# Gate and value products of a fused attention + SwiGLU kernel by Strassen's scheme

## The chip, the cores and the metric

The kernel runs on one core of a Trainium2 chip. The metric is the device time of one execution in microseconds. Engines are named as in the profile: PE (TensorE matmuls), PEld (its weight loads), DVE (VectorE), ACT (ScalarE), POOL (GpSimd), SP (SyncE, which here issues transfers).

## What is computed

Softmax attention over 8 batches of 12 heads, 448 tokens and 64 features a head, and behind it a SwiGLU block on all 3584 tokens:

```python
scores = q @ k.T / sqrt(64);  attn = softmax(scores) @ v       # per batch and head
x   = attn, heads side by side                                 # [3584, 768]
g   = x @ w_gate                                               # [768, 1536]
val = x @ w_val                                                # [768, 1536]
out = (g * sigmoid(g) * val) @ w_out                           # [1536, 768], f32 result
```

Inputs are f32; the matmuls work on f16 copies and accumulate in f32.

## The kernel before

**Attention.** Two heads make a pair; there are 48 pairs, six to a batch. The features of q and k lie on partitions (64 a head), so a score product uses half of the array's rows and the two heads of a pair sit on the two halves (tile shape 64x128 in the profile). One *unit* is one score tile of a pair for all 448 queries: two matmuls into a two-bank PSUM tile `s`, then one exp on ACT (L283), 128x896. From pair 12 on a pair has three units of 128 keys, and the 64 keys left over of two pairs share one unit (`RU`, L275, four 64x64 matmuls). The value product (`pv_mm`, L356) takes the exponentials as weights and V with a column of ones as moving operand, 65 columns; the left-over keys use 64 rows. DVE divides (L397, L398) into `xt`, and two DMA transposes on SP write the batch's columns of `X` (features on partitions, tokens along).

**SwiGLU.** For each of 12 feature tiles of 128 (`ffn1_steps`), six matmuls make the gate `gp` and six the value `vp` (L469), moving up to 512 tokens. ACT takes Tanh of half the gate (L492), DVE forms (tanh + 1) * gate (L499) and the gated product `hts` in f16 (L502). `ffn2_steps` multiplies chunks of 128 tokens by `w_out` in two halves of 384 columns, twelve matmuls each (L525); ACT evicts (L532) and SP stores. Token blocks are of 384 and 512 tokens by turns, so that all chunks are full: block 2k holds the first 384 tokens of two batches, block 2k+1 the other 512.

**PSUM.** `ps_s` has three two-bank tiles, shared by scores and gates; `ps_f` has two one-bank tiles, shared by values, value-product accumulators and output products.

**Order.** Everything is issued in one order written out by hand (`tc.manual_schedule`), and each engine works through its queue in that order. A loop over `plan` makes visits. A visit issues up to three score units in a row, then the left-over part of the value product of a pair whose units are done, for both heads, then the rest of it, and then the feature tiles and output steps due at that visit. Weights and q, k, v come through POOL's queue, cast to f16 on the way.

Of the kernel before, what the change touches and what calls it, by code (L numbers as in the profile page):

```python
# [17 lines left out]
NB = 2  # L18
# [3 lines left out]
RB = 5  # L22
# [11 lines left out]
LAST = 2  # L34
# [3 lines left out]
def kernel(  # L38
# [43 lines left out]
    raws = ctx.enter_context(tc.tile_pool(name="raws", bufs=2))  # L82
# [3 lines left out]
    fp = ctx.enter_context(tc.tile_pool(name="fp", bufs=3))  # L86
    ps_s = ctx.enter_context(tc.tile_pool(name="ps_s", bufs=3, space=PSUM))
    ps_f = ctx.enter_context(tc.tile_pool(name="ps_f", bufs=2, space=PSUM))

    Ebuf = [consts.tile([128, (NC * EB + 1) * D], FP16, name=f"E{i}") for i in range(NE)]  # L90
    Es = [e[0:P].rearrange("p (b x) -> p b x", x=D) for e in Ebuf]
    Eq = [e[:, 0 : NC * EC].rearrange("p (c x) -> p c x", c=NC) for e in Ebuf]
    Xts = [consts.tile([128, 8, D], FP16, name=f"xt{i}") for i in range(NX)]
    Vts = [consts.tile([128, 2, NC, D + 2], FP16, name=f"vo{i}") for i in range(NV)]
    vraw = consts.tile([128, VS, 2, NC, D], FP16, name="vraw")
    warm = consts.tile([128, 512], FP16, name="warm")
# [9 lines left out]

    wo = [consts.tile([128, NFB, OH], FP16, name=f"wo{i}") for i in range(2)]
# [5 lines left out]
    def dummy(n):  # L113
        wp = ps_f.tile([128, 512], FP32, tag="f", name="wp")
        for _ in range(n):
            nc.tensor.matmul(wp[:], lhsT=warm[:, 0:128], rhs=warm[:], start=True, stop=True)  # L116

    def load_qk32(pr):
        rq = raws.tile([P, 2, NC, D], FP32, tag="rq", bufs=RB)
        rk = raws.tile([P, 2, NC, D], FP32, tag="rk", bufs=RB)  # L120
        for dst, src in ((rq, q), (rk, k)):
            nc.sync.dma_start(dst[:], src[0, 2 * pr : 2 * pr + 2].rearrange("h (p c) d -> p h (c d)", c=NC))
        raw[pr] = (rq[:], rk[:])

    pairbuf = []
# [10 lines left out]


    def load_qk16(pr, n=2):
        h0 = 2 * (pr % 2) if pr >= 14 else 0
        if h0 == 0:  # L140
            q16 = raws.tile([128, 4, NC, D], FP16, tag="rq", bufs=RB, name="q16")
            k16 = raws.tile([128, 4, NC, D], FP16, tag="rk", bufs=RB, name="k16")
            pairbuf[:] = [q16, k16]
        q16, k16 = pairbuf
        for dst, src in ((q16, q), (k16, k)):
            if pr >= QUAD and dst is k16:
                kd = k16[:, ds(h0, 2 * n)].rearrange("p h c d -> p h (c d)")
                load_keys(nc.gpsimd, kd, k, 2 * pr, 2 * n)
                continue
            flat = src.rearrange("b h s d -> (b h) s d")[2 * pr : 2 * pr + 2 * n]  # L150
            nc.gpsimd.dma_start(dst[0:P, ds(h0, 2 * n)], flat.rearrange("h (p c) d -> p h (c d)", c=NC))  # L151
        for i in range(n):
            h = h0 + 2 * i
            raw[pr + i] = (q16[0:P, h : h + 2], k16[:, h : h + 2] if pr >= QUAD else k16[0:P, h : h + 2])
# [101 lines left out]

    def qk_quad(pr, c):
        s = ps_s.tile([128, 2, 512], FP32, tag="s")
        if c < KR:
# [9 lines left out]
            e = Eq[pr % NE][:, c]  # L269
        else:  # L270
# [11 lines left out]
            e = Eq[pr % NE][:, RU]  # L282
# [64 lines left out]
    def pv_mm(pr, hx, c, j):  # L347
        lo = low(pr, hx)
        first = not accs[pr][1][hx]
        accs[pr][1][hx] += 1  # L350
        if c < KR:
            rows, e, col = slice(0, 128), Eq[pr % NE][:, c], c + lo
        else:
            rows, col = (slice(0, 64), 0) if lo else (slice(64, 128), KR)
            e = Eq[(pr - pr % 2) % NE][:, RU]
        nc.tensor.matmul(  # L356
            accs[pr][0][hx][:, ts(j, D + 1)],
            lhsT=e[rows, ds(hx * S + j * 128, 128)],
            rhs=Vts[pr % NV][rows, hx, col, 0 : D + 1],
            start=first,  # L360
            stop=accs[pr][1][hx] == (KR + 1) ** 2,
        )

    def wide(pr):
        return pr >= NPAIR - LAST

    def pv_open(pr):
        if pr not in accs:
            if wide(pr):
                acc = ps_s.tile([128, 2, 512], FP32, tag="s", name="acc")  # L370
                accs[pr] = ([acc[:, 0], acc[:, 1]], [0, 0], acc)
            else:
                accs[pr] = ([ps_f.tile([128, 512], FP32, tag="f", name="acc"), ps_f.tile([128, 512], FP32, tag="f", name="acc")], [0, 0])

    def pv_piece(pr, c, heads=(0, 1)):
        pv_open(pr)
        for j in range(KR + 1):
            for hx in heads:
                pv_mm(pr, hx, c, j)

    def pv_close(pr):
        xt = Xts[pr % NX][:].rearrange("p (s h) d -> p s h d", h=2)
        if wide(pr):
            a4 = accs[pr][2][:, :, 0 : (KR + 1) * (D + 1)].rearrange("p h (s d) -> p h s d", s=KR + 1)
            r = attp.tile([128, 2, KR + 1], FP32, tag="R", bufs=4, name="R")
            nc.vector.reciprocal(r[:], a4[:, :, :, D])
            nc.vector.tensor_tensor(
                xt.rearrange("p s h d -> p h s d"),
                a4[:, :, :, 0:D],
                r[:].unsqueeze(3).to_broadcast([128, 2, KR + 1, D]),  # L390
                ALU.mult,
            )
            return
        for hx in range(2):
            a4 = accs[pr][0][hx][:, 0 : (KR + 1) * (D + 1)].rearrange("p (s d) -> p s d", s=KR + 1)
            r = attp.tile([128, KR + 1], FP32, tag="R", bufs=4, name="R")
            nc.vector.reciprocal(r[:], a4[:, :, D])  # L397
            nc.vector.tensor_tensor(  # L398
                xt[:, :, hx],
                a4[:, :, 0:D],  # L400
                r[:].unsqueeze(2).to_broadcast([128, KR + 1, D]),
                ALU.mult,
            )

    def pv_quad(pr):
        for hx in range(2):
            for c in range(KR):
                pv_piece(pr, c, (hx,))
        pv_close(pr)
# [53 lines left out]

    def ffn1_steps(kk, c0, n, hts, late=None):
        for fb in range(NFB):
# [25 lines left out]
            sg = fp.tile([128, 512], FP32, tag="sg")  # L491
# [6 lines left out]
            t1 = fp.tile([128, 512], FP32, tag="t1")  # L498
# [5 lines left out]
            )  # L504
            yield

    def ffn2_steps(kk, c0, n, hts, first, last_block):
# [6 lines left out]
        for ch, oh in steps:  # L514
# [7 lines left out]
            for m0, w in parts:  # L522
# [14 lines left out]
                l0 = c0 + ch * 128  # L537
                l = l0
                while l < l0 + 128:
                    b, j = divmod(l, S)  # L540
                    turned = D if b + NB * kk < QUAD // NHP else 0
                    c, p0 = divmod((j + turned) % S, P)
                    m = min(P - p0, l0 + 128 - l, (MQ if turned and j < MQ else S) - j)
                    eng = nc.scalar if last and m < 64 else nc.sync
                    eng.dma_start(
                        out[ts(NB * kk + b, S), :].rearrange("(p c) m -> c p m", c=NC)[
                            c, p0 : p0 + m, ds(m0, w)
                        ],
                        osb[l - l0 : l - l0 + m, ds(m0, w)],
                    )  # L550
                    l += m
            yield NFB * OH / 2400.0

    def block(i):
        kk, odd = divmod(i, 2)
        c0, n = (384, 512) if odd else (0, 384)
        hts = hp_.tile([128, NFB, 512], FP16, tag="h")
        late = (lambda: turn_x(FIRST - 1)) if i == 0 else None
        return ffn1_steps(kk, c0, n, hts, late), ffn2_steps(kk, c0, n, hts, i == 0, i == B - 1), n

    with tc.manual_schedule():
        load_qk32(0)
        nc.vector.memset(warm[:], 0.0)
        for e, eq in zip(Es, Eq):
            nc.vector.memset(eq[:, :, 2 * S :], 1.0)
            nc.vector.memset(e[:, 7::EB], 0.0)
        for vo in Vts:
# [159 lines left out]
        for x, (chunks, todo) in enumerate(plan):  # L727
# [3 lines left out]
            for _, p0 in todo:  # L731
                if p0 >= QUAD:
                    pv_piece(p0, RU)
# [37 lines left out]
            if adds[max(y for y in adds if y <= x)] < 2:  # L771
                if bare and oq and not fvq:
                    carry -= run_o()
                elif bare:
                    gate_small[0] = True
                carry = run_budget(left() / (end - x) + carry)
            else:
                nf, no = steps.pop(0) if steps else (0, 0)
                if bare and no:
                    run_o()  # L780
                    no -= 1
                elif bare:
                    gate_small[0] = True
                for y in range(nf):
                    if fvq:
                        run_fv()
                for _ in range(no):
                    run_o()
# [7 lines left out]
        oq.extend(ffn2_wait)  # L796
        ffn2_wait.clear()
        for _ in range(3):
            run_o()
        add_block(B - 1, 1)  # L800
        run_budget(1e9)
        oq.extend(ffn2_wait)
        run_budget(1e9)
# [30 lines left out]
```

## Time and profile before

| | |
|---|---|
| three timed runs | 451.52, 452.60, 452.68 us; median 452.6 |
| span of the profiled execution | 448.9 us, first to last instruction |
| between span and median | 3.7 us (launch and end; the profiled execution's own time is not listed apart) |
| PE busy | 438.8 us, 4024 matmuls |
| ACT, DVE, POOL busy | 224.9, 198.2, 180.3 us |
| gate and value matmuls (L469), output matmuls (L525) | 1152 and 684 |
| HBM read, written | 49.55 MB, 11.01 MB |

Rows of the page's groups read: line, engine, operation, output tile <- input tiles, for PE the array's tile shape (rows*columns), shape and type, count | busy us of the group, mean ns of one | idle time of the engine before them and what ended it. Matmuls are pipelined, so their mean durations overlap; what one costs in a dense stream is the distance from one start to the next. In the timeline a row is: start us, us from the first start to the last end, engine, line, operation, count.

### The profile page before, as it was taken

Reading aid. Unit: us, or ns where it says so; the run is one execution under the profiler, and the core shown is the slowest. Engines: PE = TensorE matmul, PEld = TensorE weight load, DVE = VectorE, ACT = ScalarE, POOL = GpSimd, SP = SyncE. Lnnn points to the kernel's source line nnn. Section 1 sums busy time; section 2 is a strip of 40 time slices with the busy share of each in tenths; the row PEclk is TensorE's granted clock in tenths of the full one; section 3 lists DMA queues with packets and bytes.
Section 4 is the critical chain, followed back from the end, with each engine's and each line's share of the span. In section 5 each row is a group of like instructions: output and inputs, shape, how many; then the busy total and the mean of one; then the engine's idle time right before and its main releaser. Section 6 shows DMA issues by size and latency. Waiting matters only on the chain.

```text
span 448.9 us, 9960 instructions
## 1 busy us (share of the span) xinstructions
PE 438.8 (98%) x4024; PEld 246.7 (55%) x4024; DVE 198.2 (44%) x447; ACT 224.9 (50%) x332; POOL 180.3 (40%) x299
## 2 busy tenths in 40 slices
PE   8999999899999999999999999999999999999996
PEld 3666565544455566554556556554455656644464
DVE  4666562364664354344445444343444434044400
ACT  6965666546554654455445465454454552222222
POOL 8755715997784483336444267423000000000000
PEclk9999999999999999999999999999999999999999
DMA  9999999999999799965899697955151211200033
GB/s 135 187 200 201 198 179 144 138 179 208 128 146 95 124 156 123 126 111 66 105 114 119 103 141 102 149 91 84 32 79 47 55 38 22 85 22 1 0 107 105
DMA packets 108494, 49.90 MB, mean 111 GB/s; under 512 B 60832, under 2 KB 104992, under 8 KB 108448
## 3 DMA queue, kind: packets, MB, share of 16 engines
q0 software_dynamic: 46832, 24.56, 47.6%
q1 hardware_dynamic: 61520, 24.66, 30.8%
q8 instruction: 31, 0.51, 0.5%
q14 instruction: 15, 0.12, 0.1%
q10 hardware_dynamic: 96, 0.05, 0.0%
HBM read 49.55 MB, written 11.01 MB: 135 GB/s over the span
## 4 chain that ended last, share of the span: by engine, by line
PE 76%; DMA 13%; DVE 3%; POOL 3%; ACT 2%; issue 1%; SPq 0%; DVEq 0%; POOLq 0%
PE op L525 22%; PE gp L469 22%; PE vp L469 19%; PE acc L356 8%; DMA k<-in_k_dram 5%; DMA wv<-in_moe_w_val_dram 4%; PE s L262 4%; DMA wg<-in_moe_w_gate_dram 2%; DMA qkT<-qk 2%; DVE t L499 1%; DVE hts L502 1%; ACT sg L492 1%; PE s L275 1%; ACT E L301 1%; PE wp L116 1%
## 5 line engine op out<-in xcount | busy, mean ns | idle before, releaser
L469 PE MATMUL gp<-X,wg 128*128 128x384 f16 (+1 forms) x576 | 124.8, 352 | 0.0
L469 PE MATMUL vp<-X,wv 128*128 128x384 f16 (+1 forms) x576 | 124.8, 352 | 0.0
L525 PE MATMUL op<-wo,hts 128*128 128x384 f16 (+1 forms) x684 | 115.5, 323 | 0.4 <-DVE xt L398 0.4
L283 ACT ACTIVATE E<-s 128x896 f16<-128x896 f32 x126 | 106.5, 922 | 14.9 <-PE s L262 8.7
L499 DVE SCALAR_TENSOR_TENSOR t<-sg,gp 128x384 f32<-128x384 f32 (+1 forms) x96 | 59.6, 621 | 111.7 <-ACT sg L492 111.7
L492 ACT ACTIVATE sg<-gp 128x384 f32<-128x384 f32 (+1 forms) x96 | 52.6, 548 | 92.1 <-PE gp L469 90.6
L525 PEld LDWEIGHTS <-hts 128*128 128x128 f16 x684 | 65.9, 98 | 45.6 <-issue 2.2
L469 PEld LDWEIGHTS <-wv 128*128 128x128 f16 x576 | 56.3, 98 | 52.5
L532 ACT ACTIVATE osb<-op 128x384 f32<-128x384 f32 (+1 forms) x57 | 27.6, 485 | 102.5 <-PE op L525 98.6
L469 PEld LDWEIGHTS <-wg 128*128 128x128 f16 x576 | 53.3, 98 | 45.5 <-issue 0.7
L502 DVE SCALAR_TENSOR_TENSOR hts<-t,vp 128x384 f16<-128x384 f32 (+1 forms) x96 | 59.6, 621 | 10.8 <-PE rtp L453 0.5
L188 POOL COPY qk<-k 128x512 f16<-128x512 f16 x36 | 22.9, 636 | 97.9 <-DMA qkT<-qk 95.7
L132 POOL DMA_DIRECT2D vraw<-in_v_dram x72 | 43.9, 634 | 15.2 <-DMA k<-in_k_dram 7.5
L397 DVE RECIPROCAL R<-acc 128x4 f32<-128x4 f32 x68 | 12.0, 177 | 73.9 <-PE acc L356 73.9
L356 PE MATMUL acc<-vo,E 128*128 128x65 f16 (+1 forms) x1152 | 43.0, 193 | 1.7 <-DVE hts L502 1.4
L301 ACT ACTIVATE E<-s 112x896 f16<-112x896 f32 x48 | 40.6, 916 | 7.9 <-PE s L293 7.8
L356 PEld LDWEIGHTS <-E 128*128 128x128 f16 (+1 forms) x1152 | 37.2, 96 | 12.8 <-issue 7.1
L132 POOL DMA_DIRECT2D k<-in_k_dram x70 | 42.5, 624 | 1.4 <-DMA wv<-in_moe_w_val_dram 0.8
L151 POOL DMA_DIRECT2D q<-in_q_dram x44 | 29.9, 680 | 4.7 <-PE s L293 1.5
L398 DVE TENSOR_TENSOR xt<-acc,R 128x256 f16<-128x256 f32 x68 | 28.9, 424 | 2.3
L262 PE MATMUL s<-qkT 64*128 64x448 f16 x216 | 28.1, 353 | 0.5 <-DMA qkT<-qk 0.5
L188 POOL COPY qk<-q 112x512 f16<-112x512 f16 x36 | 23.0, 639 | 0.0
(56 smaller groups left out, 184.4 us busy)
## 6 DMA issues: line engine op xcount, KB each, us to landing
vraw<-in_v_dram POOLq DMA_DIRECT2D x72, 64.0 KB, 4.7
q<-in_q_dram POOLq DMA_DIRECT2D x41, 112.0 KB, 4.0
k<-in_k_dram POOLq DMA_DIRECT2D x68, 64.0 KB, 4.7
wg<-in_moe_w_gate_dram POOLq DMA_DIRECT2D x8, 288.0 KB, 9.5
wv<-in_moe_w_val_dram POOLq DMA_DIRECT2D x8, 288.0 KB, 10.0
wo<-in_moe_w_out_dram POOLq DMA_DIRECT2D x2, 1152.0 KB, 19.8
out_dram<-osb SPq DMA_DIRECT2D x8, 288.0 KB, 3.5
out_dram<-osb SPq DMA_DIRECT2D x6, 336.0 KB, 2.9
```

The lines of the kernel that those rows point to most:

```text
L132: eng.dma_start(dst[ts(s, 64)], rows)
L151: nc.gpsimd.dma_start(dst[0:P, ds(h0, 2 * n)], flat.rearrange("h (p c) d -> p h (c d)", c=NC))
L188: nc.gpsimd.tensor_copy(dst.rearrange("p c h d -> p h c d"), src)
L262: nc.tensor.matmul(s[:, hx, 0:S], lhsT=t[ts(hx, 64), ts(c + low(pr, hx), 128)], rhs=t[ts(hx, 64), ds(NC * 128, S)], start=True, stop=True,)
L283: nc.scalar.activation(e[:, 0 : 2 * S].rearrange("p (h q) -> p h q", h=2), s[:, :, 0:S], AF.Exp, scale=sm_scale)
L301: nc.scalar.activation(e[:, :, 0:S], s[0:P, :, 0:S], AF.Exp, scale=sm_scale)
L356: nc.tensor.matmul(accs[pr][0][hx][:, ts(j, D + 1)], lhsT=e[rows, ds(hx * S + j * 128, 128)], rhs=Vts[pr % NV][rows, hx, col, 0 : D + 1], ...
L469: nc.tensor.matmul(dst[:, 0:n], lhsT=wslice(kind, fb, cb), rhs=X[kk][:, cb, ds(c0, n)], start=(cb == 0), stop=(cb == NCB - 1),)
L492: nc.scalar.activation(sg[:, 0:n], gp[:, 0:n], AF.Tanh, scale=0.5)
L499: nc.vector.scalar_tensor_tensor(t1[:, 0:n], sg[:, 0:n], 1.0, gp[:, 0:n], ALU.add, ALU.mult)
L502: nc.vector.scalar_tensor_tensor(hts[:, fb, 0:n], t1[:, 0:n], 0.5 * HS, vp[:, 0:n], ALU.mult, ALU.mult)
L525: nc.tensor.matmul(op[:, 0:w], lhsT=hts[:, fb, ts(ch, 128)], rhs=wo[oh][:, fb, ds(m0 - oh * OH, w)], start=(fb == 0), stop=(fb == NFB - 1),)
```

## The change

From batch 2 on the blocks are whole batches of 448 tokens, and the visits end. The gate and value products of feature tiles 0 to 8 of these six batches are made by Strassen's scheme in Winograd's form: the 2x2 grid is (features: two halves of 384) x (tokens: two halves of 224) against (gate, value); seven products of three matmuls each, 224 columns wide, take the place of eight. Four sums of weights per tile are formed once, on DVE, during batch 1 (`weight_sums`; one of them over the value weights themselves, the others into what were parts of the `E` and raw q/k buffers). Four sums of the tokens are formed per batch on DVE (`token_sums`). Feature tiles 9 to 11 stay plain.

A tile goes in four stages. Stage 1: two products into bank `g[0]`, then DVE copies the first into bank `g[1]`, ACT copies the second to SBUF (`p5`). Stage 2: a product is accumulated on the copy in `g[1]` and one on `g[0]`; DVE adds `p5`. Stage 3: one more product on each bank, another add, Tanh. Stage 4: the last product, then the two DVE steps as before. Two tiles are interleaved: stages 3 and 1 of neighbours share a half slot, 4 and 2 the other. After each half slot `fill` issues at most one score unit with the value products due after it (one head at a time), by turns with output pieces of four feature tiles.

PSUM from there: one two-bank tile `s`, two pairs of banks `g`, `small[0]` for outputs and `small[1]` for value products. The 64 tokens that a batch leaves over are made as two 64-row output pieces side by side, for the two column halves of `w_out`.

The diff, cut to its core (buffers of raw q/k, of E, and the early pool layout are changed as well):

```diff
+    def weight_sums(fb):
+        ...
+        nc.vector.tensor_sub(s3, g[:, lo, f], v[:, lo, f])
+        nc.vector.tensor_add(v[:, lo, f], v[:, lo, f], v[:, hi, f])
+        nc.vector.tensor_sub(s2, v[:, lo, f], g[:, lo, f])
+        nc.vector.tensor_sub(s4, g[:, hi, f], s2)
+    def token_sums(i):
+        ...
+        nc.vector.tensor_sub(t1, x12, x11)
+        nc.vector.tensor_sub(t2, x22, t1)
+        nc.vector.tensor_sub(t3, x22, x12)
+        nc.vector.tensor_sub(t4, x21, t2)
     def ffn1_steps(...):
         ...
+            if c0 and fb < SP * len(Ssum):
+                weight_sums(fb)
+    class Group:
+        def product(self, dst, w, x, first=False):
+            for c in sums:                       # three matmuls (L604 of after)
+                nc.tensor.matmul(dst, lhsT=w(c), rhs=x(c), ...)
+        ...
+        def stage1(self):
+            ...
+            self.product(g[0][:, 0:HB], self.ww("g", 0), self.xx(0, 0), True)
+            self.product(g[0][:, HB:S], lambda c: wslice("v", self.fb, c), self.xt(0))
+            nc.vector.tensor_copy(g[1][:, 0:HB], g[0][:, 0:HB])
+            self.p5 = fp.tile([128, HB], FP32, tag="p5", name="p5")
+            nc.scalar.activation(self.p5[:], g[0][:, HB:S], AF.Copy)
+        def stage2(self):
+            ...
+            self.product(g[1][:, 0:HB], self.wm(0), self.xt(1))
+            self.product(g[0][:, 0:HB], self.ww("g", 1), self.xx(1, 0))
+            nc.vector.tensor_add(g[0][:, HB:S], g[1][:, 0:HB], self.p5[:])
+        def stage3(self):
+            ...
+            self.product(g[1][:, 0:HB], self.wm(1), self.xt(2))
+            self.product(g[0][:, HB:S], self.wm(2), self.xx(1, 1))
+            nc.vector.tensor_add(g[1][:, HB:S], g[1][:, 0:HB], self.p5[:])
+            self.tanh()
+        def stage4(self):
+            if self.summed:
+                self.product(self.g[1][:, 0:HB], self.ww("v", 1), self.xt(3))
+    def out_items(i, banks):
+        ...
+                if ch is None:                   # the 64 tokens left over
+                    for oh in range(2):
+                        nc.tensor.matmul(op[ts(oh, 64), 0:OH], lhsT=hts[:, fb, ds(n - n % 128, 64)], rhs=wo[oh][:, fb], ...)
+        ...
+        for f0 in range(0, NFB, PC):             # PC = 4: pieces of four feature tiles
+            items.append(lambda f0=f0: piece((ch, m0), m0, w, f0, f0 + PC, ch))
     ...
-        for x, (chunks, todo) in enumerate(plan):
+        for x, (chunks, todo) in enumerate(plan[:start]):     # until batch 2
     ...
+        held["s"] = ps_m.tile([128, 2, 512], FP32, name="s")
+        gs = [[ps_m.tile([128, 512], FP32, name=f"g{i}{x}") for x in "ab"] for i in range(2)]
+        small = [ps_m.tile([128, 512], FP32, name=f"small{i}") for i in range(2)]
+        for _, g in gs:
+            nc.tensor.matmul(g[:], lhsT=warm[:], rhs=warm4, start=True, stop=True)       # L987
+        def pv_head(pr, hx):
+            for c in (RU, *range(KR)):
+                pv_piece(pr, c, hx)
+            pv_close(pr, hx)
+        ...
+        def fill(n, want, outs, n_out):
+            todo = att.pop(0) if att and n_att - len(att) < n else []
+            while todo or n_out - len(outs) < want:
+                if todo:
+                    todo.pop(0)()
+                if n_out - len(outs) < want:
+                    outs.pop(0)()
+        prev = None
+        token_sums(BS)
+        for i in range(BS, B):
+            ...
+            for fb in range(NFB):
+                cur = Group(i, fb, hts, gs[(i * NFB + fb) % 2])
+                for half in range(2):
+                    if half == 0:
+                        if prev:
+                            prev.stage3()
+                        cur.stage1()
+                    else:
+                        if prev:
+                            prev.stage4()
+                        cur.stage2()
+                        if prev:
+                            prev.swish()
+                            prev.gated()
+                    ...
+                    fill(n_att * pos // att_slots, want, outs, n_out)
+                prev = cur
+                if fb == len(Ssum) * SP and i + 1 < B:
+                    token_sums(i + 1)
```

## The prediction

> **What bounds the kernel now.** I read the page first (shares, slices, chain), then the list of waits, then the groups by shape, and last a short timeline of PE, because the first three say that only PE's own stream matters.
>
> ```profile
> span 448.9 us, 9960 instructions
> PE 438.8 (98%) x4024; PEld 246.7 (55%) x4024; DVE 198.2 (44%) x447; ACT 224.9 (50%) x332; POOL 180.3 (40%) x299
> ...
> PEclk9999999999999999999999999999999999999999
> ...
> PE 76%; DMA 13%; DVE 3%; POOL 3%; ACT 2%; issue 1%; SPq 0%; DVEq 0%; POOLq 0%
> ...
> PE acc L356 <- DVE hts L502: 1.4, 7, 0.2
> ```
>
> PE is busy 98% of the span at the full granted clock, and 261.22 of the 262 us between 130 and 392 (busy time by stretches). The longest entry of PE's matmuls in the list of waits is the last line: 1.4 us over the whole span. So a microsecond put into or taken out of PE's stream is a microsecond of the span. How long is each piece of that stream?
>
> ```profile
> L525 PE MATMUL op<-wo,hts 128*128 128x384 f16 x660 | 113.5, 326 | 0.4 <-DVE xt L398 0.4
> ...
> L398 DVE TENSOR_TENSOR xt<-acc,R 128x256 f16<-128x256 f32 x68 | 28.9, 424 | 2.3
> ...
> L525 PE MATMUL op<-wo,hts 128*128 128x192 f16 x24 | 2.1, 246 | 0.0
> ...
> L237 DVE CAST qkT<-tp 128x224 f16<-128x224 f32 x2 | 0.8, 391 | 0.4 <-PE tp L229 0.4
> ...
> L238 ACT ACTIVATE qkT<-tp 128x224 f16<-128x224 f32 x2 | 0.7, 357 | 0.7 <-DVE qkT L237 0.7
> ```
>
> Mean durations of matmuls overlap, so I take spacing. In the chain of waits six 512-column matmuls take 1.29 us (0.2157 each) and twelve 384-column ones 1.95 (0.1625). That is 0.416 ns a column and about 3 ns per instruction. For 192 columns it gives 0.083, and the 24 of them, busy 2.1 us with a last one of 0.246, are (2.1 - 0.246)/23 = 0.081 apart. So a short matmul still hides its weight load, and I may interpolate: 224 columns cost 0.096 us, 448 cost 0.189.
>
> Now the seams between kinds of matmul:
>
> ```profile
> 257.09 0.49 PE L525 MATMUL op<-wo,hts 128*128 128x384 f16 x2
> 257.51 0.38 PE L275 MATMUL s<-qkT 64*64 64x448 f16 x4
> 257.83 0.55 PE L262 MATMUL s<-qkT 64*128 64x448 f16 x4
> 258.31 0.34 PE L525 MATMUL op<-wo,hts 128*128 128x384 f16 x1
> ...
> 187.38 2.11 PE L525 MATMUL op<-wo,hts 128*128 128x384 f16 x12
> 189.42 0.74 PE L262 MATMUL s<-qkT 64*128 64x448 f16 x6
> 190.00 1.18 PE L356 MATMUL acc<-vo,E 64*128 64x65 f16 x32
> ```
>
> Two output products from 257.09 fill the array until 257.09 + 2 x 0.1625 = 257.415; the next kind starts at 257.51, 0.095 later. Two pairs of 64-row scores from 257.83 end at 257.83 + 2 x 0.189 = 258.21; the output product after them starts at 258.31, 0.10 later. From 187.38, twelve products end at 189.33 and the scores start at 189.42. But three pairs of scores end at 189.99 and the first value products (L356, also 64x128) start at 190.00: same shape, no gap. So **each change of the array's tile shape costs PE about 0.095 us**, both ways. In before, a visit pays this seldom: three score units, then both heads' 64-row value products, then full-array work.
>
> **The change, part by part.**
>
> *Columns.* A feature tile of a batch took 12 matmuls of 384 or 512 columns: 12 x (0.1625 + 0.2157)/2 = 2.27 us. Strassen's takes 7 products of 3 matmuls of 224: 21 x 0.096 = 2.02. Nine of twelve tiles in six batches: 54 x 0.253 = **-13.7 us**. The three plain tiles cost the same as before (12 x 0.189 = 2.27).
>
> *Shape changes.* In the PE instruction order of the two programs I counted neighbouring matmuls of different tile shape: 180 before, 410 after. From full array to scores 69 -> 133, scores back to full 30 -> 104 (units are now handed out one per half tile, each between full-array products, where three stood together); value products of 64 rows entered from full or column-tiled work 1 -> 50, left 36 -> 65 (a head is now taken alone and no longer directly behind scores); the rest are the quarter-array scores and the column-tiled pieces, the half chunks of 64 tokens among them. 230 x 0.095 = **+21.9 us**.
> A rule of the Trainium skill is weighed here: "TensorEngine Tiling (Array Packing)", Key Properties, says that a change of tiling mode, not of tile, drains TensorE. It speaks against this change, but gives no price; were the drain a matmul's whole latency beyond its slot (0.326 - 0.1625 = 0.164, an estimate), it would be +37.7. The seams above show 0.095, and I go by them.
>
> *Value products of 64 rows.* The two heads of a pair sat on different halves of the rows and ran two at a time (eight in some 0.12 us); one head alone runs its four in a row, 8 x 0.029 = 0.23 per pair. 36 pairs: **+4 us**.
>
> *Half chunks.* The 448 tokens of a batch leave 64: 24 matmuls of 64 weight columns, two at a time. If the pairs run together, 12 x 0.1625, as half a chunk pair cost before: 0. The 112-column transposes (L252, also 64 weight columns) support it: 180 of them are busy 8.1 us, 0.045 each and below the 0.050 of one alone by the slope above, waits included. If they did not, 6 x 1.95 = +11.7; I take 0. The two clearing products (L987) are +0.4.
>
> PE's stream: -13.7 + 21.9 + 4 + 0.4 = **+12.6 us**.
>
> *New waits.* (a) DVE forms 36 weight sums (128x384, 16-bit, SBUF) in batch 1, queued behind each gated product and ahead of the next tile's. No row shows the operation. The rows of 256 and 512 f32 elements from PSUM (L398 424 ns, L387 690 ns) give 1.04 ns an element and 0.157 fixed: 0.56 us for 384. The 16-bit copy of 960 (L253, 657 ns) gives 0.52 an element, half as much: 0.36. "VectorE: DVE Perf Modes", the perf-mode tier table, gives tensor_tensor on 16-bit SBUF data the double rate (1224 ns for 2048), so by it 0.36; no run here shows it. I take 0.36 by the 16-bit copy row: 13 us (up to 20) on top of 19.9 busy in the 35 us from 95 to 130, where PE's accumulators already wait for hts. DVE would be 94 to 114% full: +2.5, range 0 to 8.
> (b) In each Strassen tile PE waits on DVE three times and on ACT once. The tightest: stage 3 may not touch the bank until the add of stage 2 is done. The Tanh rows start some 0.04 after the last matmul's row (0.16 beyond its slot), so 0.20 + 0.39 (the 224-element row) + 0.06 = 0.65 us. Its cover is what is filled in behind stage 2: four output products, 4 x 0.1625 = 0.65, and mostly a score unit of 0.38 besides. So it is hidden but for the first slots of a batch and a few in batch 7, which have no filling: some 10 x 0.3. Behind a wait, all of PE's queue stands. The p5 copy (0.357) delays the next exp on ACT; with one score buffer left (L293 of after) the next unit needs 0.2 + 0.92 + 0.06 after its predecessor, and half a tile lasts 1.6 us or more. Token sums (24, 0.5 to 0.9 us) stand at tile 9, whose plain products cover them. DVE as a whole goes from 112 to some 180 of 262 us. Together +3, range -3 (the waits of before gone) to +15.
> SP and POOL: 146 transposes stay; stores on SP grow from 58 to 64; nothing moves past the path.
>
> Sum: +12.6 + 2.5 + 3 = +18.1. The span goes from 448.9 to 467.0; 3.7 us lie between span and the median of 452.6, which I keep: **470.7 us**.
>
> **Rivals.**
> 1. *Shape changes are hidden* (the faster side). If an isolated unit lets the seam overlap, say because its weights are loaded early, the price drops from 0.095. Then 452.6 - 13.7 + 4.4 + 5.5 = 448.8. It decides for faster below (13.7 - 4.4 - 5.5)/230 = 0.017 us a change (0.04 without new waits). Against it: both directions show the same price wherever PE waits for nothing else. 0.05.
> 2. *DVE and ACT become the bound.* Per tile the loop add, swish, gated, add, copy, product is 0.39 + 0.62 + 0.62 + 0.39 + 0.39 + some 0.5 = 2.9 us against 3.3 of PE in batch 7 and 4.5 elsewhere. If handoffs or DVE's queue cost 0.3 us more at each of 54 tiles, +16 on top of the forecast: 485 to 490. 0.13.
> 3. *No difference*: gains and seams cancel (0.04 a change, no waits): 0.02. That the change doesn't do what it says is excluded by the order: 1134 = 54 x 21 matmuls of 224 columns.
>
> **How the numbers follow.** The forecast, PE's stream longer by its seams, has 0.80; its own range is 452.6 + 12.6 - 3 = 462 to 452.6 + 12.6 + 8 + 10 = 483. With part of rival 2 in, the range is 461 to 485. A measurement of this kernel can tell about 0.3%, 1.4 us: faster 0.05, same 0.02, slower 0.93.
>
> **What would show it.** Right: PE still over 95% busy between 130 us and the end; L604 near 0.096 apart; gaps of 0.095 at each score unit between L604 and L711; the last batch's part without attention shorter than before's. Wrong: gaps near zero at these seams (rival 1), or large totals of "PE g <- DVE" in the waits and PE below 93% (rival 2).

## The result, and the profile after

| | before | after |
|---|---|---|
| median of the timed runs | 452.64 us (451.52 to 453.03) | 483.61 us (483.03 to 485.37) |
| ratio, 95% interval | | 1.0704 [1.0667, 1.0740] |
| span of the profiled execution | 448.9 us | 481.8 us |
| that execution's own time | not listed | 483.57 us |

The change costs 31.0 us, where 18.1 were forecast. The page of the changed kernel, the lines that answer to those shown of before:

```profile
span 481.8 us, 11421 instructions
...
PE 459.8 (95%) x4584; PEld 290.7 (60%) x4584; DVE 280.3 (58%) x674; ACT 246.8 (51%) x386; POOL 182.3 (38%) x301
...
PE   8999998988889999999999999999999998989996
...
PEclk9999998999999999999999999999999999999999
...
PE 81%; DVE 11%; DMA 3%; ACT 2%; issue 1%; SPq 1%; DVEq 0%
```

PE is still what the kernel waits for, but it has two kinds of loss now. Its busy time grew by 21 us (438.8 to 459.8), although the columns that it works through became fewer; and its busy share fell from 98% to 95%. The slices show where: 8s early, between a fifth and a third of the span, and near the end. The share of DVE in the chain that ended last went from 3 to 11%.

To separate the two I add up each program's matmuls in their order on PE by the spacing of their starts: 0.417 ns a column and 2.5 ns an instruction (in after 224 columns start 0.096 us apart, 512 columns 0.216), tiles that lie side by side together, and 0.095 us at each change of tile shape. This sum is called *stream*. Whatever the trace's last matmul start lies beyond first start + stream is called *waits* (a slower clock counts among them).

| kernel | shape changes | stream us | waits us | span us | ratio to before [95%] |
|---|---|---|---|---|---|
| before | 180 | 428.5 | 15.5 | 448.9 | |
| after | 410 | 441.1 | 35.9 | 481.8 | 1.0704 [1.0667, 1.0740] |
| seam64 | 408 | 452.0 | 16.2 | 473.1 | 1.0508 [1.0471, 1.0546] |
| seam128 | 180 | 430.3 | 16.5 | 451.8 | 1.0038 [1.0006, 1.0070] |
| todo_first | 320 | 432.5 | 34.6 | 471.8 | 1.0487 [1.0417, 1.0557] |
| plain_tiles | 410 | 455.0 | 20.9 | 480.4 | 1.0663 [1.0618, 1.0709] |
| no_weight_sums | 410 | 441.1 | 29.8 | 475.5 | 1.0565 [1.0525, 1.0605] |
| keys_joined | 410 | 441.1 | 35.2 | 481.0 | 1.0701 [1.0673, 1.0728] |
| fine_fill | 420 | 442.0 | 46.1 | 493.3 | 1.0947 [1.0896, 1.0997] |
| last_two | 204 | 427.2 | 35.4 | 467.3 | 1.0389 [1.0367, 1.0411] |
| plain_todo_first | 320 | 446.4 | 19.1 | 469.9 | 1.0471 [1.0432, 1.0509] |
| last_two_spread | 202 | 427.0 | 25.6 | 457.4 | 1.0163 [1.0135, 1.0191] |

The kernel before had medians of 451.8, 450.5 and 451.3 us beside the three groups of experiments, so kernels of different groups are compared by their ratios.

After against before: stream +12.6 and waits +20.4 make the two profiled spans differ by 32.9 us. The medians differ by 31.0: some 2 us of the new waits are a stretch of slower clock that the profiled execution of before happens not to have (see the 3.7 us in the section on the prediction). The seams can be read off the trace. The timeline of PE after:

```profile
220.59 0.45 PE L604 MATMUL g1a<-T,wv 128*128 128x224 f16 x3
220.98 0.36 PE L299 MATMUL s<-qkT 64*128 64x448 f16 x2
221.27 0.82 PE L711 MATMUL small<-wo,hts 128*128 128x384 f16 x4
221.93 0.45 PE L604 MATMUL g0b<-T,wv 128*128 128x224 f16 x3
```

Three products of 224 columns take 3 x 0.096 = 0.29 us and end at 220.88; the score unit starts 0.10 later. Its pair takes 0.189, to 221.17; the output products start 0.10 later. They end at 221.27 + 4 x 0.1625 = 221.92, and the next Strassen product follows at once, because the shape is the same.

### The profile page after: what moved, and what is told of

It reads as the page before. It is cut to its first block, busy times and chain, and to the rows that moved or that the text cites. A ratio compares the mean times of both kernels' runs of the same rounds, so it can differ in the third digit from the quotient of the medians.

```text
span 481.8 us, 11421 instructions
## 1 busy us (share of the span) xinstructions
PE 459.8 (95%) x4584; PEld 290.7 (60%) x4584; DVE 280.3 (58%) x674; ACT 246.8 (51%) x386; POOL 182.3 (38%) x301
## 4 chain that ended last, share of the span: by engine, by line
PE 81%; DVE 11%; DMA 3%; ACT 2%; issue 1%; SPq 1%; DVEq 0%
PE small L711 19%; PE small L390 8%; PE g0a L604 7%; PE g1a L604 5%; PE g0b L604 5%; PE s L299 5%; PE g1b L604 4%; PE gp L504 3%; PE small L702 3%; PE g1a L628 3%; PE g1b L628 3%; DMA qkT<-qk 3%; PE vp L504 2%; PE s L329 2%; PE acc L355 2%; PE op L577 2%
## 5 line engine op out<-in xcount | busy, mean ns | idle before, releaser
L711 PE MATMUL small<-wo,hts 128*128 128x384 f16 (+1 forms) x540 | 105.1, 324 | 0.6 <-ACT osb L726 0.6
L206 POOL COPY qk<-qkraw 128x512 f16<-128x512 f16 x72 | 43.8, 646 | 119.8 <-DMA qkT<-qk 117.9
L711 PEld LDWEIGHTS <-hts 128*128 128x128 f16 x540 | 46.0, 98 | 38.0 <-issue 16.5
L390 PE MATMUL small<-vo,E 128*128 128x65 f16 (+1 forms) x928 | 44.2, 193 | 1.6 <-DVE vo L187 0.9
L148 POOL DMA_DIRECT2D qkraw<-in_k_dram x72 | 43.5, 619 | 3.0 <-DMA wg<-in_moe_w_gate_dram 1.6
L604 PEld LDWEIGHTS <-E 128*128 128x128 f16 x324 | 29.5, 97 | 8.3 <-issue 6.2
L504 PE MATMUL vp<-X,wv 128*128 128x384 f16 (+1 forms) x144 | 31.4, 353 | 1.7 <-DVE xt L411 1.7
L604 PEld LDWEIGHTS <-wv 128*128 128x128 f16 x324 | 29.3, 98 | 5.3 <-issue 2.4
L604 PEld LDWEIGHTS <-wg 128*128 128x128 f16 x324 | 31.3, 98 | 1.7 <-issue 0.2
L169 POOL DMA_DIRECT2D qkraw<-in_q_dram x44 | 29.8, 678 | 6.2 <-DMA vraw<-in_v_dram 1.9
L504 PE MATMUL gp<-X,wg 128*128 128x384 f16 (+1 forms) x144 | 31.4, 353 | 0.0
L604 PE MATMUL g0a<-X,wg 128*128 128x224 f16 x180 | 27.0, 259 | 0.0
```

What stands on the lines that cost most here:

```text
L148: eng.dma_start(dst[ts(s, 64)], rows)
L169: nc.gpsimd.dma_start(dst, flat.rearrange("h (p c) d -> p h (c d)", c=NC))
L206: nc.gpsimd.tensor_copy(dst.rearrange("p c h d -> p h c d"), src)
L390: nc.tensor.matmul(acc[:, ts(j, D + 1)], lhsT=e[rows, ds(hx * S + j * 128, 128)], rhs=Vts[pr % NV][rows, hx, col, 0 : D + 1], start=first, ...
L504: nc.tensor.matmul(dst[:, 0:n], lhsT=wslice(kind, fb, cb), rhs=X[kk][:, cb, ds(c0, n)], start=(cb == 0), stop=(cb == NCB - 1),)
L604: nc.tensor.matmul(dst, lhsT=w(c), rhs=x(c), start=first and c == 0, stop=c == NCB // 2 - 1, skip_group_check=True,)
```

## Experiments

Two theories stood at the outset. *Theory A* (the prediction's): the loss is shape changes plus a few waits of the new scheme. *Theory B*: a seam as such is cheap, and the loss is handoffs between PE and DVE/ACT, in the Strassen tiles above all.

### seam64 and seam128: the price of a shape change by itself

Kernel before, with two tiny matmuls (32 columns) added to each run of twelve output products, once with 64 rows (the shape changes and changes back) and once with 128 (it doesn't). They add 114 matmuls over zeros to output sums that stay the same.

```diff
+                    if fb in (3, 7):
+                        nc.tensor.matmul(op[:, 0:32], lhsT=warm[0:64, 0:128],   # seam128: warm[0:128]
+                            rhs=warm[0:64, 0:32], start=False, stop=False)
```

> The kernel before, with 114 added matmuls of 32 columns by zero weights on 64 rows, two in each output step, so that the array's shape changes 228 times more (180 to 408) and nothing else moves; the sums stay what they were. Seam theory: 228 x 0.095 = 21.7 us, plus some 114 x 0.02 = 2 us for the matmuls themselves, so 452.6 + 23.5 = 476. Handoff theory (seams overlap, the loss of the changed kernel is waiting for DVE and ACT): as its twin with 128 rows, 453 to 456.

> The twin: the same 114 added matmuls, on all 128 rows, so that the array's shape does not change (180 changes as before). Both theories: 114 x 0.016 to 0.03 us = 2 to 3.5 us, so 454.5 to 456. The price of a change of shape is the difference of the two runs divided by 228.

Measured: 475.13 us (474.84 to 475.48) and 453.46 us (452.65 to 455.91), beside 451.8 for before. The two differ by the 64 or 128 rows of the added matmuls alone, and so by 228 shape changes: 21.67 / 228 = **0.095 us a change**. The timeline of PE in seam64:

```profile
448.12 0.19 PE L533 MATMUL op<-warm 64*128 64x32 f16 x1
448.24 0.82 PE L525 MATMUL op<-wo,hts 128*128 128x384 f16 x4
448.99 0.19 PE L533 MATMUL op<-warm 64*128 64x32 f16 x1
449.11 1.15 PE L525 MATMUL op<-wo,hts 128*128 128x384 f16 x6
```

and in seam128:

```profile
426.04 0.81 PE L525 MATMUL op<-wo,hts 128*128 128x384 f16 x4
426.69 0.18 PE L533 MATMUL op<-warm 128*128 128x32 f16 x1
426.72 0.81 PE L525 MATMUL op<-wo,hts 128*128 128x384 f16 x4
```

In seam64 four products from 448.24 end at 448.89, and the small one starts at 448.99. It needs 0.016 for its columns, and the next full-array product starts at 449.11: 0.10 into the other shape and 0.10 back. In seam128 the small one starts at the end of the four (426.69), and 0.03 later the next does. No DVE or ACT handoff is involved, so theory B falls for this part.

### todo_first: fewer seams, same work

The changed kernel, but the attention work of a fill is issued together ahead of the output pieces, not by turns with them. Scores and 64-row value products then stand side by side, with no seam between them.

```diff
-            while todo or n_out - len(outs) < want:
-                if todo:
-                    todo.pop(0)()
-                if n_out - len(outs) < want:
-                    outs.pop(0)()
+            while todo:
+                todo.pop(0)()
+            while n_out - len(outs) < want:
+                outs.pop(0)()
```

> The changed kernel with one reordering: between half tiles the score unit and the value products due after it go first, and the output pieces behind them, where they went by turns. The 64-row value products then follow the scores in the same shape: 410 changes of shape become 320, all instructions are the same. Seam theory: PE's stream falls by 8.7 us (90 x 0.095), time 483.6 - 8.7 = 475, plus or minus 2 for waits that move. Handoff theory: no fewer waits, 482 to 486.

Measured: 474.77 us (470.3 to 476.9). 90 changes fewer come to 8.55 us; the medians differ by 8.8, the streams by 8.6. The timeline of PE:

```profile
220.48 0.36 PE L299 MATMUL s<-qkT 64*128 64x448 f16 x2
220.68 0.75 PE L390 MATMUL small<-vo,E 64*128 64x65 f16 x16
221.27 0.81 PE L711 MATMUL small<-wo,hts 128*128 128x384 f16 x4
```

The value head starts 0.20 after its scores, which need 0.189. So some 9 of the 31 us come from the turn-taking in `fill` alone, and Strassen's scheme doesn't need it.

### plain_tiles: the new order without Strassen's scheme

The changed kernel, all twelve feature tiles plain, no sums.

```diff
-            if c0 and fb < SP * len(Ssum):
-                weight_sums(fb)
...
-            self.summed = fb // SP < len(Ssum)
+            self.summed = False
...
-        token_sums(BS)
```

> The changed kernel with all twelve feature tiles of the six batches plain (no weight sums, no token sums, no Strassen stages); same order, same PSUM layout, 410 changes of shape. Seam theory: PE's stream is 455.1 us by the rows (13.9 more than with Strassen), and the waits on the Strassen handoffs and on the weight sums (some 14 us of the 20 new ones) fall away: 483.6 + 13.9 - 14 = 481 to 486, so that Strassen's saving and its waits cancel and the loss is the order's. Handoff theory: all the loss sits in the Strassen stages, so the time comes back to 453 to 462.

Measured: 482.18 us (481.74 to 482.46), 0.3% under the changed kernel's 483.61. From its page:

```profile
span 480.4 us, 10044 instructions
...
PE 468.2 (97%) x4098; PEld 244.4 (51%) x4098; DVE 196.7 (41%) x452; ACT 228.0 (47%) x332; POOL 181.1 (38%) x301
```

PE is busy 8.4 us longer than after and yet done 1.4 us earlier. In the sums: Strassen's scheme takes 13.9 us out of the stream (455.0 to 441.1) and puts 15.0 into the waits (20.9 to 35.9). **All that the changed kernel loses against before is in the plain order around the tiles**: seams, unpaired value products, and 5.4 us of waits (20.9 against 15.5), some 1.5 of them slower clock (below).

### no_weight_sums: what the sums of batch 1 cost

The sums of weights are left out, and the three products that need them use plain gate weights of the same shape (that part of the computation is changed); all matmuls, handoffs and token sums stay.

```diff
-            if c0 and fb < SP * len(Ssum):
-                weight_sums(fb)
...
-            return lambda c: Ssum[piece][:, m, c, ds(off * 128, 128)]
+            return lambda c: wslice("g", self.fb, c)
```

> The changed kernel without the 36 weight sums on DVE in batch 1: the three products that use them take the plain gate weights in their place (so this part of the computation is left out), and PE's order and shapes are the same. If DVE's queue in batch 1 causes the waits between 100 and 142 us (6.6 us there against some 2 in the kernel before), they fall to about 2: 483.6 - 4.5 = 479. If these waits come from the scores' transposes or from PSUM, nothing changes: 483 to 484.

Measured: 476.06 us (474.74 to 478.32). By the ratios that is 0.0139 x 452.6 = 6.3 us less than after; by the waits 6.0 (35.9 to 29.8). Of these, 5.2 lie between 95 and 160 us (8.8 to 3.6 of waits); the sums run from 94 to 128. Another 1.0 has come up by 95 us, up to where the two kernels issue the same but for the first sums, so that it is the difference of two executions. Busy time from 95 to 130 us (length, then PE, PEld, DVE, ACT and POOL, each with its count, granted clock, DMA share, GB/s), after:

```profile
95.00:130.00 35.00, 30.93 (x263) 14.80 (x262) 31.46 (x72) 17.91 (x24) 29.20 (x49) 1.00 1.37 150
```

and in no_weight_sums:

```profile
95.00:130.00 35.00, 34.55 (x313) 17.43 (x312) 20.01 (x45) 20.48 (x27) 29.68 (x52) 1.00 1.45 165
```

With the sums DVE is 90% busy, and PE is held up for 3.6 us more and gets through 50 matmuls fewer in the same stretch. The list of waits of after names the queue:

```profile
PE vp L504 <- DVE xt L411: 1.7, 2, 1.1
...
PE s L299 <- DVE t L534: 1.4, 2, 0.9
```

The divide `xt` (L411) and the gate step `t` (L534) stand behind the sums in DVE's queue; the accumulator or score buffer that they free is what PE needs next.

Neither entry is in the list of waits of no_weight_sums.

With plain_tiles, this splits the 15.0 us: **5.2 to 6.0 for the weight sums, 8.9 for the handoffs of the Strassen tiles** (29.8 - 20.9; the token sums on DVE are in this part).

### keys_joined: the stall at 75 us

The page's slices and the timeline of after show a stall, and a slow stretch behind it:

```profile
74.79 0.37 PE L311 MATMUL s<-qkT 64*64 64x448 f16 x1
76.67 0.38 PE L311 MATMUL s<-qkT 64*64 64x448 f16 x3 [1.51 <-DMA qkT<-qk]
...
78.59 3.64 PE L577 MATMUL op<-wo,hts 128*128 128x384 f16 x12
```

Twelve output products took 3.64 us, not some 2.1, right after PE had waited 1.5 us for keys. The fresh theory was that the split load of k brings the keys too late. The edit loads the keys of four heads with one transfer again where the changed kernel used two.

```diff
+            if pr >= QUAD and t and n == 2:
+                kd = raws_all[:, pr % RS // 2, 1].rearrange("p b (h x) -> p (b h) x", h=2)
+                load_keys(nc.gpsimd, kd, k, 2 * pr, 4)
+                continue
```

> The changed kernel with the keys of pairs 12 to 15 loaded as in the kernel before, two pairs in one transfer of 128 KB (four transfers less on POOL's queue of 0.6 us each). If the stall at 75 us (1.9 us at the first left-over score, and output products at half the clock behind it, some 1.4 us) comes from these transfers, 483.6 - 3 = 480.5. If it comes from the other changes of the early part (buffers, memsets, a later start), 483 to 484.

Measured: 482.55 us (480.92 to 483.57), ratio 1.0701: not told apart from after. The timeline of PE:

```profile
75.66 2.12 PE L581 MATMUL op<-wo,hts 128*128 128x384 f16 x12
...
79.83 0.37 PE L303 MATMUL s<-qkT 64*128 64x448 f16 x2 [1.09 <-DMA qkT<-qk]
```

The stall at 75 us and the slow twelve are gone: by 78 us the waits are 2.8 us fewer than in after. But the next keys are late at 79.8, and by 142 us 0.8 of the gain is lost. Another 1.5 goes at 402 us, where PE works at half clock for 3.4 us in this execution and not in after (last section). At the end 0.7 is left. A miss for the theory that taking this stall away wins its length. Nor is the split load shown to be its cause. todo_first and plain_todo_first load the keys in two transfers, issue the same as after up to 75 us, and have no wait for keys in their lists; last_two, with joined keys, waits longer than after did. From its list:

```profile
PE s L303 <- DMA qkT<-qk: 2.0, 1, 2.0
```

So the keys come late in some executions and not in others.

### fine_fill: output pieces of two tiles, not four

```diff
-PC = 4
+PC = 2
```

> The changed kernel with output pieces of two feature tiles instead of four (PC = 2), so that hardly a half slot of the last batch stays without filling; 420 changes of shape, PE's stream 0.9 us longer. If the waits of batch 7 (7.3 us from 395 on, none in the kernel before) come from slots with no filling, some 3 to 4 us of them go: 483.6 + 0.9 - 3.5 = 481. If DVE's own rate is the limit there, they stay: 484.5.

Measured: 493.86 us (491.70 to 496.17), 10 us slower than after where a gain was expected. From its list of waits:

```profile
PE small L711 <- ACT osb L726: 8.3, 10, 1.0
```

In after the same entry is 0.6 us, once. A finer piece lets the end of one output step and the start of the next fall into one fill. Both go through the single bank `small[0]`, so PE stands until ACT has evicted it, 0.99 us in one case. The expectation had counted PE's stream and the waits of batch 7, and left out that bank.

### plain_todo_first: both edits

plain_tiles and todo_first together (the two diffs above).

> plain_tiles and todo_first together: no Strassen, score units and value products handed out together, 320 changes of shape. PE's stream by the rows 446.4 us. If Strassen's saving of 13.9 us is eaten by its own waits in any order, 482.2 - 8.7 = 473.5, the same as todo_first with Strassen (474.8). If Strassen's waits were a matter of the fill's order, todo_first would be ahead by several us: 478 or more here.

Measured: 472.28 us (471.42 to 473.79); todo_first with Strassen's tiles had 474.77, the ratios are 1.0471 and 1.0487. With 90 seams fewer Strassen's scheme still brings nothing: stream 446.4 to 432.5, waits 19.1 to 34.6 (the profiled execution of todo_first has a stretch of half clock at 116 us, that of plain_todo_first none). The 21 us that plain_todo_first loses to before are the order's: stream +17.9, waits +3.6.

### last_two and last_two_spread: Strassen only where little attention is left

Here the new order begins with batch 6, not 2, so most of the visits with their few seams stay. The weight sums move to batch 5. The left-over part of a pair's value products keeps its pairing, the fill is that of todo_first, keys are joined, `PC = 2`, and the last outputs take the two small banks in the other order.

```diff
-BS = 2
+BS = 6
-            if c0 and fb < SP * len(Ssum):
+            if c0 and kk == BS // NB - 1 and fb < SP * len(Ssum):
...
-                    for hx in range(2):
-                        pv_piece(p0, RU, hx)
+                    for j in range(KR + 1):
+                        for hx in range(2):
+                            pv_mm(p0, hx, RU, j, accs[p0][hx], j == 0, False)
...
-        for f in out_items(B - 1, small):
+        for f in out_items(B - 1, small[::-1]):
```

> Strassen and the new order for batches 6 and 7 alone (BS = 6, weight sums in batch 5), with the reordering of todo_first, the left-over value products of two heads by turns in the visits, joined keys, PC = 2, and the last output pieces on the other bank first. 204 changes of shape; PE's stream by the rows is 427.3 us, 1.3 less than in the kernel before. Seam theory: 427.3 + 16.7 of waits as before + 2 to 6 new ones + 7.5 us at the end = 453 to 458, no gain of a size that can be told. Were the seams not what it costs, 18 tiles x 0.253 = 4.6 us less than before: 447 to 449.

Measured: 468.42 us (467.51 to 469.05), 10 us above the top of what was expected. The stream was as worked out, 1.3 us *below* before's (427.2 against 428.5), but the waits were 35.4. From the list of waits:

```profile
PE op L581 <- DVE xt L415: 3.0, 8, 0.4
PE acc L394 <- DVE hts L541: 3.0, 12, 0.4
```

The changed kernel hands out the feature tiles of the visits ahead of batch 2 by a budget, not by before's list of steps per visit; over two batches this costs little, over six the accumulators and outputs meet in `ps_f` again and again: 26.8 of the 35.4 us lie ahead of the first Strassen product. So before's steps were put back (and `PC = 4`):

```diff
+            else:
+                nf, no = steps.pop(0) if steps else (0, 0)
+                ...
+                for y in range(nf):
+                    if fvq:
+                        run_fv()
+                for _ in range(no):
+                    run_o()
```

> last_two with PC = 4 again and the visits' output steps of batches 2 to 5 spread as in the kernel before. 202 changes of shape, PE's stream 427.1 us by the rows. last_two stood 18 us above the kernel before with 35 us of waits, where that kernel has 15.5. If the visits' spreading and the fine pieces made these, the waits fall to 15.5 plus 5 to 8 for batches 6 and 7: 427.1 + 22 + 6.5 of start and end = 454 to 458. If the two Strassen batches themselves make them, 464 to 468.

Measured: 458.84 us (458.01 to 459.48), ratio 1.0163 [1.0135, 1.0191]: 0.8 above the top of the range of the spreading theory. The waits fell from 35.4 to 25.6, and 8.8 of that lies ahead of the first Strassen product (26.8 to 18.0), where `PC` plays no part. It is the best of all versions with Strassen's tiles, but still slower than before. None of the kernels run beats the one before. Its waits exceed before's by 10.1 us, in the main from 360 us on (7.4 against 0.1), where the Strassen tiles are.

## Why the prediction was right, and where it was too low

The direction, the seams and the stated range held: 483.6 lies within 461 to 485, but 13 us above the forecast of 470.7, only 1.4 under the top, and just outside the 462 to 483 that the forecast had without a part of rival 2. PE's stream, which the forecast took for most of the loss, is 12.6 of the 31.0 us; the new waits, put at 5.5, came to 18.4. That the range still held is in part luck: terms (a) and (b) both came out in the upper part of theirs. Point by point:

- **PE's stream, +12.6: right.** The same rows over both programs give 441.1 - 428.5 = 12.6. The seam was tested by runs: 0.095 to 0.10 a change in the trace, 0.0950 between seam64 and seam128, 8.8 us for todo_first's 90. The columns rest on the rows, L604 at 0.096 in the trace; plain_tiles has 13.9 more in the stream, where 13.7 had been worked out. The 4 us of value products one head at a time were not run apart. The drain of "TensorEngine Tiling (Array Packing)", Key Properties, is thus confirmed in kind, and the estimate of 0.164 made from it, not.
- **Half chunks at 0: right.** The groups by shape:

```profile
L702 PE MATMUL small<-wo,hts 128*64 128x384 f16 x144 | 14.8, 331 | 0.6 <-ACT osb L726 0.6
```

  Eight of them in a fill hold PE for 0.65 us, four times 0.1625, so the pairs run side by side.
- **Term (a), the weight sums, +2.5 (0 to 8): mis-sized, 5.2 to 6.0.** The operation was priced well: 36 sums took 16.9 us of DVE, between the 13 and 20 named, and undisturbed ones 0.35 to 0.36 each, as the 16-bit copy row had it. The tier table of "VectorE: DVE Perf Modes" had given 0.36 too. What failed is the step from DVE's load to PE's wait: I had taken a DVE near 94 to 114% as nearly hidden. At a mean of 90% the divides already come late, since the sums stand in bursts of four ahead of them.
- **Term (b), handoffs and layout, +3 (-3 to +15): mis-sized, 8.9 + 5.4 = 14.3, or some 12.4 without the slower clock.** The price of a bare handoff was nearly right. An unfilled slot of batch 7 in the timeline of after:

```profile
421.32 0.45 PE L604 MATMUL g0a<-X,wg 128*128 128x224 f16 x3
...
421.88 0.40 DVE L665 TENSOR_TENSOR g0a<-g0b,p 128x224 f32<-128x224 f32 x1 [1.00 <-PE g0a L604]
...
422.33 0.45 PE L604 MATMUL g0b<-T,E 128*128 128x224 f16 x3 [0.56 <-DVE g0a L665]
```

  The product fills PE until 421.61, stage 3 starts at 422.33: 0.72 us, where 0.65 had been worked out. The count was too low. "Some 10 x 0.3" put the loss into the first slots and batch 7; comparing no_weight_sums with plain_tiles, waits from 360 us on are 8.4 against 3.3, which is that part, but from 160 to 360, taken as covered, they are 6.2 against 3.0. And 0 had been set for the layout itself. In plain_tiles, where no Strassen handoff is left, the list of waits has 0.7 us for a value head on the one bank `small[1]`, 1.2 for output steps on `small[0]` and 0.9 for the two clearing products; some 1.5 of the 5.4 is half clock behind the stall for keys.
- **"Nothing moves past the path" on SP and POOL: wrong in one point.** POOL's copies of q and k run beside the weight sums and hold them up (last section): the 36 sums take 16.9 us, against 12.8 in last_two, where no copy runs beside them. What these 4.1 us of DVE cost PE wasn't tried. The stall at 75 us comes and goes with the execution.
- **The 3.7 us between span and median: harmless, but not all launch and end.** The later profiled executions lie 1.7 to 1.8 us above their spans (483.57 against 481.8 after). So the profiled execution of before, at full granted clock (1.000), stands for some 450.7 us; the rest, 1.9, is slower clock in other executions. Of the 27 executions of before beside the experiments, those with a granted clock of 0.999 or 1.000 took 449.8 to 451.9 us, those with 0.992 to 0.996 took 452.7 to 455.4. All four of after have 0.993 to 0.996. The forecast added its 18.1 to the median of before and so lost nothing by it; but the traces of after and before differ by these 2 us beside the change, and with them 12.6 + 6.0 + 12.4 = 31.0.
- **Rivals.** 1 (seams hidden) falls by seam64. 2 named 485 to 490, 1.4 us above the result and far nearer than the forecast, by a mechanism that is half there: waits on DVE grew, but the entries "PE g <- DVE" of the Strassen tiles in the list of waits come to 4.2 us and PE stayed at 96.3% between 130 us and the end (338.8 of 351.8), above the 93% named. DVE and ACT aren't the bound. 3 is out.
- **Signs.** L604 0.096 apart and gaps of 0.095 at the score units were there as named. The "last part without attention" couldn't be read: the new order leaves other work for it.

What stays open: the split of the 8.9 us of handoffs between DVE's three steps and ACT's copy wasn't tried by itself, and no run gave the outputs or the value products a second small bank.

## What to carry to other kernels

Fewer matmul columns are worth nothing until the order that they need is priced: count the neighbouring matmuls of unlike tile shape in both programs, at 0.095 us each here, before counting what is saved. Run the new order with the old arithmetic (plain_tiles) early; here it showed at once that the order lost it all and that the scheme paid for its own waits and no more. An engine at 90% with bursts, or one single-buffered bank on the way, delays its neighbour well before its mean load reads full.

## What was not expected of the hardware

A sum of weights on DVE is slowed by a copy on POOL. The timeline of after:

```profile
118.43 1.69 DVE L484 TENSOR_TENSOR wv<-wv 128x384 f16<-128x384 f16 x1
118.67 1.22 POOL L206 COPY qk<-qkraw 128x512 f16<-128x512 f16 x2
...
120.22 0.36 DVE L485 TENSOR_TENSOR qkraw<-wv,wg 128x384 f16<-128x384 f16 x1
```

The sum that shares its time with two copies takes 1.69 us, the next one 0.36. Of the 36 sums 13 overlap a POOL copy (median 646 ns, up to 1690); the other 23 take 351 to 360 but for one of 467. In last_two none of them overlaps one, and all take 350 to 360. The same group of nine (mean ns behind the busy time) in after:

```profile
L484 DVE TENSOR_TENSOR wv<-wv 128x384 f16<-128x384 f16 x9 | 5.7, 634 | 0.3
```

and in last_two:

```profile
L488 DVE TENSOR_TENSOR wv<-wv 128x384 f16<-128x384 f16 x9 | 3.2, 358 | 0.3
```

In ten of the 13 a copy is already running when the sum starts, and the sum ends 207 to 225 ns after that copy, whatever it took until then.

The Trainium skill's "SBUF — State Buffer", in its section "SBUF: two separate sides", says that DVE and GpSimd share a port pair as an exclusive lock, that whichever starts first holds it for a whole instruction, and that the other is blocked. The ten rows agree. The row at 118.43 doesn't in one point: its sum starts 0.24 us ahead of the first copy and still ends 0.22 after the second. A run that takes POOL's copies alone away was not made.

The second: in seven of the traces (after and six of the experiments) PE's granted clock falls to half once in the middle of the program, for 3.4 us. In after this is the stretch behind the wait for keys, where twelve output products took 3.64 us, against 2.12 in keys_joined (the granted clock is the third figure from the end):

```profile
74.87:78.28 3.41, 1.90 (x35) 1.06 (x36) 0.00 (x0) 1.71 (x4) 3.41 (x7) 1.00 0.87 127
78.28:81.69 3.41, 3.41 (x21) 1.81 (x18) 1.03 (x3) 1.35 (x2) 3.41 (x7) 0.50 1.54 135
```

In keys_joined that wait is gone, and the stretch lies behind two waits of value heads:

```profile
400.54 0.75 PE L394 MATMUL small<-vo,E 64*128 64x65 f16 x16 [0.88 <-DVE vo L191]
402.02 1.15 PE L394 MATMUL small<-vo,E 64*128 64x65 f16 x16 [0.73 <-DVE xt L415]
...
398.61:402.02 3.41, 1.80 (x22) 1.08 (x23) 2.35 (x6) 0.92 (x1) 0.00 (x0) 1.00 0.17 34
402.02:405.44 3.42, 3.42 (x29) 2.82 (x29) 0.93 (x3) 0.54 (x1) 0.00 (x0) 0.50 0.13 26
```

In all seven PE had been busy for only 1.4 to 1.9 us of the 3.4 ahead of the stretch. In after the wait of 1.5 us is thus followed by another 1.5 that twelve products took longer. That the wait is the cause is read from the order in time and not from an experiment, and not every such wait does it: fine_fill, with 1.83 of 3.40 us busy from 136.8 on, kept its full clock.
